# Side value blocks of a decode kernel: eight-way loads from the Pool engine's queue instead of five-way loads from SP's

## The chip, the core and the metric

The kernel runs on one core of a Trainium2 chip. A core has a matrix engine (PE), a vector engine (DVE), a scalar engine (ACT), a general engine (POOL, also called GpSimd), a sync engine (SP) that here only issues transfers, and sixteen DMA engines that move data from the device's memory into the on-chip memory of 128 partitions. The metric is the device time of one execution in microseconds (us); lower is better.

## The reference

Two layers over two sequences, one new token each: layer norm, grouped-query attention over a cache of 32768 keys, residual, layer norm, a gated feed-forward (ReGLU), residual. All in 32-bit floats.

```
def A(x, k_cache, v_cache, wq, wo):          # Hq 32, Hkv 8, rep 4, Dh 128, Sk 32768, D 512
    q = (x @ wq).reshape(B, Sq, Hq, Dh).transpose(0, 2, 1, 3)
    k, v = jnp.repeat(k_cache, rep, axis=1), jnp.repeat(v_cache, rep, axis=1)
    scores = jnp.einsum("bhqd,bhkd->bhqk", q, k) * (Dh ** -0.5)
    o = jnp.einsum("bhqk,bhkd->bhqd", softmax(scores, axis=-1), v)
    return o.transpose(0, 2, 1, 3).reshape(B, Sq, Hq * Dh) @ wo
def B(x, W_gate, W_up, W_down):              # F 1792
    gate, up = x @ W_gate, x @ W_up
    return ((gate * (gate > 0)) * up) @ W_down
x = x + A(_layernorm(x), k_cache, v_cache, wq, wo);  x = x + B(_layernorm(x), W_gate, W_up, W_down)
x = x + A(_layernorm(x), k_cache, v_cache, wq, wo);  x = x + B(_layernorm(x), W_gate, W_up, W_down)
```

The two caches are 1 GB of the 1.1 GB that an execution reads: 16 pairs of a head group and a sequence, each with 16.8 MB of keys and 16.8 MB of values in each layer. The output is two rows of 512 numbers.

## The kernel before

The order of all work is written out by hand; no scheduler changes it. A layer has sixteen turns, one for each pair of key-value head and sequence. Turn `i` scores its keys (`keys(i)`, matmuls `sc`, line 218), then multiplies the values of turn `i - 1` (`values(i - 1, ...)`, matmuls `acc`, line 304) while the softmax of turn `i` runs on DVE and ACT. The second layer walks the turns in the reverse order, and takes a part of the first layer's last keys and values from on-chip memory, where they were kept (`kept_k`, `kept_v`).

Nearly all loads go into one large buffer, `arena`, of 221 units of 256 numbers in each partition. `take(width)` gives a piece of it, `done(...)` returns it; the piece that was returned longest ago is used first, so that a load waits for the work which used that piece last and for the load that filled it. All loads are issued by SP, in the order of the program (line 76). SP waits until the first load in its queue may start; whatever stands behind waits with it.

Keys and values of a turn are eight pages (`j` 0 to 7) of 4096 numbers a partition, 2 MB each. In most turns four pages come with one transfer of 64 KB a partition; in the last two turns of a layer values come page by page. A transfer over 128 partitions is split evenly over the sixteen DMA engines, and each engine takes its shares in the order of issue, so that a page is there when the last engine has finished.

A page of values is eight blocks of 512 numbers a partition: each block holds 128 keys by 4 chunks, and is multiplied by 16 columns of transposed probabilities `pT`. In one turn of each layer, turn 14 (`SIDE_TURNS`), page 3 is loaded without its last three blocks (width 2560), and these three blocks come apart, out of an array `side` that the host has laid out anew from the same values: two transfers (`load_side`, line 292) over 20 partitions each, whose source has an outer dimension of 5. Their keys stand in other partitions than in the page. `side_keys` (lines 269 to 273) therefore makes a second set of transposed probabilities for them, and `v_side` (line 280) multiplies them: ten matmuls behind those of page 3.

Pool has little to do: two powers for the norm of the queries (line 193), and the clearing of a few buffers.

Of the kernel before, what the change touches and what calls it, by code (L numbers as in the profile page):

```python
# [7 lines left out]
F32 = mybir.dt.float32  # L8
# [4 lines left out]
P = 128  # L13
D = 512
# [3 lines left out]
NG = HKV * NB  # L18
NT = 8
# [5 lines left out]
NLAYER = 2  # L25
# [3 lines left out]
PIECE = 256  # L29
PAGE = 4096  # L30
HALF = 4
UNITS = 221
TOP = 192
SCRATCH = 64


KEPT_PAGES = (4, 5, 6)
# [8 lines left out]
C_SAME, C_MEAN, C_SEL, C_PAIR, C_SIDE, C_ONE, C_MHALF, C_END = 0, 128, 160, 192, 224, 225, 226, 228  # L46


@with_exitstack
def attention_reglu_decode(ctx: ExitStack, tc: tile.TileContext, x, k, v, wq, wo, wgu, wd, consts, side, out):  # L50
    nc = tc.nc
    sb = ctx.enter_context(tc.tile_pool(name="sb", bufs=1))
# [21 lines left out]
    def load(src, top=False):  # L74
        t = take(src.shape[-1], top, False)
        nc.sync.dma_start(t[0], src)
# [38 lines left out]
    selh = sel[:, :16]  # L115
    col = sel[:, :NB]
    pair = cst[:, C_PAIR : C_PAIR + 32]
    side_rows = cst[:, C_SIDE : C_SIDE + 1]
# [122 lines left out]
    def soft_tail(L, n, aside=False):  # L241
        p, rs = red_of.pop(n)
        pT = take(2 * D)
        for B in range(2):
            nc.vector.transpose(pT[0][:, B * D : (B + 1) * D], p[0][:, B * D : (B + 1) * D])  # L245
        if aside:
            side_of[n] = side_keys(p[0])
        done(p)
        sm = small(f"sm{L}_{n}")
        nc.tensor.matmul(sm[:, 0:1], same, rs, start=True, stop=True)  # L250
        linv = one()
        nc.vector.reciprocal(linv, sm[:, 0:1])  # L252
        pT_of[n], linv_of[n] = pT, linv
# [2 lines left out]


    def side_keys(p):
        W = SIDE_CHUNKS * 32
        t = take(2 * W)  # L260
        at = SIDE_PAGE // 2 % 2 * D + (SIDE_PAGE % 2 * 8 + 8 - SIDE) * 32

        def windows(rows):
            return bass.AP(rows.tensor, rows.offset + at, [rows.ap[0], [SIDE_ROWS, SIDE_CHUNKS], [1, 32]])

        def chunks(rows):
            return rows.rearrange("p (k r) -> p k r", r=32)

        nc.gpsimd.memset(t[0][64:, W:], 0.0)
        nc.vector.transpose(chunks(t[0][:, :W]), windows(p))  # L270
        for c in (0, 32):
            nc.vector.transpose(chunks(t[0][c : c + 32, W:]), windows(p[64 + c : 96 + c]))
        nc.vector.tensor_scalar_mul(t[0], t[0], side_rows[:, 0:1])
        return t

    def v_side(n, vt):
        t = side_of.pop(n)
        J = SIDE_PAGE // 4
        for k in range(2 * SIDE_CHUNKS):
            nc.tensor.matmul(  # L280
                acc[32 * (k % 4) : 32 * (k % 4) + 16, :],
                t[0][:, 32 * k + 16 * J : 32 * k + 16 * J + 16],
                vt[:, k * D : (k + 1) * D],
                start=False, stop=False,
            )
        done(t)

    def load_side(at):
        W = 2 * SIDE_CHUNKS * D
        t = take(W, False, False)  # L290
        for c in range(2):
            nc.sync.dma_start(t[0][32 * c : 32 * c + SIDE_ROWS], side[at, c, :, : 4 * W].rearrange("e (r f) -> e r f", r=4))
        return t


# [1 line left out]
    def v_tile(n, j, vt, first, last, blocks):  # L297
        pT = pT_of[n][0].rearrange("p (b m r) -> p b m r", m=16, r=32)
        parts = 4 // len(blocks) if len(blocks) < 4 else 1
        for at, ch in enumerate(blocks):  # L300
            J, B, m = j // 4, j // 2 % 2, j % 2 * 8 + ch
            for e in range(parts):
                c, w = (ch + e * len(blocks)) % 4, D // parts
                nc.tensor.matmul(  # L304
                    acc[32 * c : 32 * c + 16, e * w : (e + 1) * w],
                    pT[:, B, m, 16 * J : 16 * J + 16],
                    vt[:, at * D + e * w : at * D + (e + 1) * w],
                    start=first and ch < 4, stop=last and blocks[-1] == 7 and at >= len(blocks) - 4,
                )

    acs_of = {}
# [78 lines left out]
    for L in range(NLAYER):  # L390
        last = L == NLAYER - 1
        seq = list(range(NG)) if L % 2 == 0 else list(range(NG - 1, -1, -1))

        def keys(i):
            n = seq[i]
            if i < NG - 1:
                place_queries(i + 1, seq[i + 1])
            if last and i == 0:
                loads = list(kept_k)
                kept_k.clear()  # L400
            else:
                loads = pages(k, n, not (last and i == 1))
            for j, t in enumerate(loads):
                k_tile(L, i, n, j, t[0])
                if not last and i == NG - 1:
                    kept_k.append(t)
                else:
                    done(t)
                if last and i == 0:
                    yield  # L410
                if j == 1 and i >= 1:
                    soft_tail(L, seq[i - 1], i - 1 in SIDE_TURNS)
                if j == 2 and i >= 2:
                    head_out(L, seq[i - 2])
                    if i % 2 == 1:
                        project(load(wo[seq[i - 2] // NB], True), i == 3, False)


        def values(i, soft):
            n = seq[i]  # L420
            whole = (j for j in ())
            if i == NG - 1:
                pieces = [(j, 0, 8, None) for j in range(NT - 1)]
                pieces += [(NT - 1, h, h + 2, None) for h in range(0, 8, 2)]
                if not last and KEPT_FROM < 8:
                    pieces[KEPT_PART : KEPT_PART + 1] = [(KEPT_PART, 0, KEPT_FROM, None), (KEPT_PART, KEPT_FROM, 8, None)]
            elif last and i == 0:
                pieces = kept_v[1:] + kept_v[:1]
                pieces += [(j, 0, 8 if j != KEPT_PART else KEPT_FROM, None) for j in range(NT) if j not in KEPT_PAGES]
                kept_v.clear()  # L430
            else:
                pieces = [(j, 0, 8, None) for j in range(NT)]
                if i in SIDE_TURNS:
                    pieces[SIDE_PAGE] = (SIDE_PAGE, 0, 8 - SIDE, None)
                elif i < NG - 2:
                    whole = pages(v, n, True)
            for at, (j, lo, hi, t) in enumerate(pieces):
                t = t or next(whole, None) or load(v[n, j // HALF, :, j % HALF * PAGE + lo * D : j % HALF * PAGE + hi * D])
                v_tile(n, j, t[0], at == 0, j == NT - 1, range(lo, hi))
# [6 lines left out]
                if i in SIDE_TURNS and j == SIDE_PAGE:  # L446
                    t_side = load_side(len(SIDE_TURNS) * L + SIDE_TURNS.index(i))
                    v_side(n, t_side[0])
                    done(t_side)
# [73 lines left out]
```

## Time and profile before

| | |
|---|---|
| median of three runs | 2586.75 us (2586.34 to 2587.0) |
| the profiled execution | 2585.52 us, span of its instructions 2583.7 us |
| read from memory | 1105.39 MB, 428 GB/s over the span |
| packets of the DMA engines | 31446, of which 31204 from SP's queue, 75 of instructions |
| chain that ended last | DMA 69%, PE 22%, unknown 8% |
| SP waited at the side pieces (line 292) | 42.4 us once for values, 10.5 for keys, 4.8 and 2.1 for PE |

Times in the profile count from the first instruction of the span. A row of a table by stretches gives the stretch, its length, the busy time of each engine with the number of instructions, the clock that PE was granted, the mean busy share of the sixteen DMA engines (1.00 is all of them, all of the time; a packet counts where it starts, so short stretches can lie a little beside the truth), and the GB/s. In rows of work, "SPq" is SP issuing a transfer, "PEld" is PE loading weights, and "[2.41 <-DMA arena<-side]" says that the engine sat idle for 2.41 us until that transfer had landed. A PE matmul of the program is two in the profile.

### The profile page before, as it was taken

The numbers are of one execution on the slowest core, as the hardware profiler recorded it, in microseconds if no ns is written. First come the engines' busy times: TensorE is split into PE (matmuls) and PEld (weight loads), VectorE is DVE, ScalarE is ACT, GpSimd is POOL, SyncE is SP. The second block draws the span as 40 slices with busy tenths as digits, with TensorE's granted clock in tenths as the row PEclk, the third lists the DMA queues.
The fourth block names the chain that finished last, engine by engine and source line by source line (L and its number), as shares of the span: only waits on it lengthen the run. The fifth ranks groups of instructions, "written<-read, shape, count | busy, mean of one in ns | idle before, by whom it ended". The sixth has DMA issues, their size and how long they took to land.

```text
span 2583.7 us, 20190 instructions
## 1 busy us (share of the span) xinstructions
PE 1322.4 (51%) x9588; PEld 351.7 (14%) x9588; DVE 148.4 (6%) x357; ACT 40.9 (2%) x67; POOL 2.4 (0%) x10
## 2 busy tenths in 40 slices
PE   3554554455455445545685454445445544554465
PEld 1111111111111111111121111111111111111111
DVE  0000000000000000000010000000000000000000
ACT  0000000000000000000000000000000000000000
POOL 0000000000000000000000000000000000000000
PEclk9777777777777777777777777777777777777787
DMA  9999999999999999999999999999999999999999
GB/s 423 436 426 433 436 430 433 437 428 435 431 436 427 436 437 427 434 434 403 414 387 438 428 433 435 434 430 436 431 430 437 433 426 437 435 430 434 431 424 376
DMA packets 31446, 1106.75 MB, mean 428 GB/s; under 512 B 3500, under 2 KB 3764, under 8 KB 6836
## 3 DMA queue, kind: packets, MB, share of 16 engines
q1 hardware_dynamic: 31204, 1105.34, 99.5%
q8 instruction: 75, 1.23, 0.2%
q10 hardware_dynamic: 160, 0.12, 0.0%
q14 instruction: 7, 0.06, 0.0%
HBM read 1105.39 MB, written 0.07 MB: 428 GB/s over the span
## 4 chain that ended last, share of the span: by engine, by line
DMA 69%; PE 22%; another core or an unknown queue 8%; DVE 0%; issue 0%; ACTq 0%; SPq 0%; POOL 0%; DVEq 0%; POOLq 0%
DMA arena<-k 45%; DMA arena<-v 21%; PE sc L218 14%; PE acc L304 5%; DMA cst<-consts 1%; DMA arena<-wgu 1%; PE qp L186 1%; PE po L326 1%; DMA arena<-wq 1%; PE op L166 1%; PE gu L345 0%; PE dn L371 0%; PE mp L232 0%; PE sm L250 0%
## 5 line engine op out<-in xcount | busy, mean ns | idle before, releaser
L304 PE MATMUL acc<-arena 128*16 128x512 f32 (+1 forms) x4116 | 593.0, 727 | 598.5 <-DMA arena<-v 598.5
L218 PE MATMUL sc<-arena,qz 128*32 128x512 f32 x4096 | 591.6, 730 | 592.6 <-DMA arena<-k 592.6
L218 PEld LDWEIGHTS sc<-arena,qz 128*32 128x32 f32 x4096 | 143.4, 130 | 987.8 <-issue 664.9
L304 PEld LDWEIGHTS acc<-arena 128*16 128x16 f32 x4116 | 118.5, 109 | 1023.1 <-issue 512.4
L228 DVE TENSOR_REDUCE stat<-sc 128x1 f32<-128x1024 f32 x32 | 39.2, 1225 | 662.4 <-PE sc L218 662.4
L238 ACT ACTIVATE arena<-sc,stat 128x1024 f32<-128x1024 f32 x32 | 35.6, 1113 | 2360.2 <-DVE stat L235 2308.2
L320 DVE TENSOR_SCALAR arena<-acc,stat 128x512 f32<-128x512 f32 (+1 forms) x38 | 24.8, 665 | 810.6 <-PE acc L304 810.6
L245 DVE STREAM_TRANSPOSE arena<-arena 128x512 f32<-128x512 f32 x64 | 41.5, 687 | 2.4 <-ACT arena L238 2.4
L326 PE MATMUL po<-cst,arena 128*128 128x4 f32 x256 | 34.7, 258 | 2.1 <-DVE arena L320 2.1
L326 PEld LDWEIGHTS po<-cst,arena 128*128 128x128 f32 x256 | 31.9, 195 | 26.7 <-issue 23.5
L252 DVE RECIPROCAL stat<-sm 128x1 f32<-128x1 f32 x32 | 5.3, 166 | 415.4 <-PE sm L250 415.4
L345 PE MATMUL gu<-arena 128*32 128x448 f32 x128 | 22.7, 836 | 9.5 <-DMA arena<-wgu 9.2
L235 DVE TENSOR_REDUCE stat<-mp 128x1 f32<-128x32 f32 x32 | 6.1, 191 | 350.1 <-PE mp L232 350.1
L186 PE MATMUL qp<-arena 128*32 128x512 f32 x128 | 22.7, 822 | 5.7 <-DMA arena<-wq 3.0
L166 PE MATMUL op<-arena,oT 128*2 128x128 f32 x512 | 18.3, 287 | 4.1 <-DVE oT L329 4.1
L232 PEld LDWEIGHTS mp<-arena,cst 128*128 128x128 f32 x64 | 13.1, 256 | 52.1 <-issue 49.6
L145 PE MATMUL meana<-cst,stat 128*128 128x32 f32 x4 | 1.0, 341 | 35.5 <-DMA cst<-consts 35.0
L232 PE MATMUL mp<-arena,cst 128*128 128x32 f32 x64 | 16.9, 353 | 3.5 <-DVE arena L231 3.5
L250 PEld LDWEIGHTS sm<-stat,cst 128*128 128x128 f32 x64 | 9.5, 188 | 28.4 <-issue 28.4
L166 PEld LDWEIGHTS op<-arena,oT 128*2 128x2 f32 x512 | 12.3, 87 | 6.4 <-DVE oT L329 5.5
L250 PE MATMUL sm<-stat,cst 128*128 128x1 f32 x64 | 12.2, 260 | 0.0
L329 DVE COPY oT<-po 128x4 f32<-128x4 f32 x32 | 5.1, 161 | 76.4 <-PE po L326 76.4
(56 smaller groups left out, 94.1 us busy)
## 6 DMA issues: line engine op xcount, KB each, us to landing
arena<-v SPq DMA_DIRECT2D x31, 2048.0 KB, 27.7
arena<-wo SPq DMA_DIRECT2D x16, 1024.0 KB, 51.2
arena<-k SPq DMA_DIRECT2D x8, 2048.0 KB, 16.8
arena<-wq SPq DMA_DIRECT2D x8, 1024.0 KB, 8.5
arena<-wgu SPq DMA_DIRECT2D x8, 896.0 KB, 7.9
arena<-wgu SPq DMA_DIRECT2D x4, 1792.0 KB, 21.0
arena<-v SPq DMA_DIRECT2D x8, 512.0 KB, 34.2
arena<-wd SPq DMA_DIRECT2D x4, 1024.0 KB, 8.7
```

The costliest lines, as they stand in the source:

```text
L166: nc.tensor.matmul(tot[32 * c : 32 * c + rows.shape[-1], :P], rows, w[:, c * P : (c + 1) * P], start=start, stop=stop)
L186: nc.tensor.matmul(qp[32 * c : 32 * c + 32, B, :], xT[:, kt, :], t[0][:, c * D : (c + 1) * D], start=kt == 0, stop=kt == KT - 1)
L218: nc.tensor.matmul(sc_of[n][32 * c : 32 * c + 32, B, :], qz[:, i % 2, 28 - 4 * j : 60 - 4 * j], kt[:, ch * D : (ch + 1) * D], start=j == 0 ...
L228: nc.vector.tensor_reduce(m1, sc_of[n], AX.XY, ALU.max)
L232: nc.tensor.matmul(mp[:, :32], same, mt[0], start=True, stop=True)
L238: nc.scalar.activation(p[0], sc_of[n].rearrange("p a b -> p (a b)"), AF.Exp, bias=nm[:, 0:1], scale=1.0, accum_out=rs)
L245: nc.vector.transpose(pT[0][:, B * D : (B + 1) * D], p[0][:, B * D : (B + 1) * D])
L250: nc.tensor.matmul(sm[:, 0:1], same, rs, start=True, stop=True)
L304: nc.tensor.matmul(acc[32 * c : 32 * c + 16, e * w : (e + 1) * w], pT[:, B, m, 16 * J : 16 * J + 16], vt[:, at * D + e * w : at * D + (e + ...
L320: nc.vector.tensor_scalar_mul(acs[:, at : at + w], acc[:, at : at + w], linv[:, 0:1])
L326: nc.tensor.matmul(po[:, :REP], acs[0][:, t * P : (t + 1) * P], selh[:, 4 * t : 4 * t + 4], start=t == 0, stop=t == 3)
L345: nc.tensor.matmul(gu[32 * j : 32 * j + 32, s, :FS], xT[:, kt, :], t[0][:, j * FS : (j + 1) * FS], start=kt == 0, stop=kt == KT - 1)
```

## The change

Turn 14 of each layer now leaves the last three blocks out of two pages, 3 and 7, so that there are six side blocks a layer. They keep the keys' partitions modulo 64: partitions 0 to 63 hold the blocks of the page's lower half and, beside them, those of its upper half. For the lower half `pT` is used as it is, and for the upper half `side_keys` transposes two small pieces of 32 x 96.

The side pieces are now issued by Pool (`nc.gpsimd.dma_start`), whose transfers go through a queue that software on Pool fills. Each page's side blocks come in two transfers over 32 partitions, whose source has an outer dimension of 8. In front of each stands a transfer of a few numbers into a buffer of its own, `turned`, by `steer`: with 13 groups the first time, with 8 each time after. The change counts on Pool's queue giving the groups of a transfer to as many DMA engines, starting behind the one where the transfer before ended: 13 engines, then 8 for side data, then always 8 and 8, so that the side data is always on the same eight.

The scratch memory that such a queue needs grows from 64 to 512, and `arena` loses one unit. The column of constants that `side_keys` used falls away.

```
-UNITS = 221
+UNITS = 220
-SCRATCH = 64
+SCRATCH = 512
-SIDE_TURNS = (14,)
-SIDE_PAGE, SIDE = HALF - 1, 3
-SIDE_ENGINES, SIDE_ROWS, SIDE_CHUNKS, SIDE_GAP = 5, 20, 5, 64
+SIDE_TURN = NG - 2
+SIDE_PAGES, SIDE = (3, 7), 3
+SIDE_ROWS, SIDE_GAP, BEFORE, AROUND = 64, 64, 13, 8
...
     def side_keys(p):
...
-        nc.gpsimd.memset(t[0][64:, W:], 0.0)
-        nc.vector.transpose(chunks(t[0][:, :W]), windows(p))
+        B, m = SIDE_PAGES[0] // 2 % 2, SIDE_PAGES[0] % 2 * 8 + 8 - SIDE
+        at = B * D + m * 32
+        t = take(SIDE * 32)
         for c in (0, 32):
-            nc.vector.transpose(chunks(t[0][c : c + 32, W:]), windows(p[64 + c : 96 + c]))
-        nc.vector.tensor_scalar_mul(t[0], t[0], side_rows[:, 0:1])
+            nc.vector.transpose(t[0][c : c + 32], p[64 + c : 96 + c, at : at + SIDE * 32])
         return t
...
+    turned = sb.tile([P, 4], F32, name="turned")
+    whole_turn = [BEFORE, AROUND]
+    def steer():
+        n = whole_turn[0] if len(whole_turn) > 1 else AROUND
+        if len(whole_turn) > 1:
+            whole_turn.pop(0)
+        few = consts[: 5 * n, :4].rearrange("(e r) f -> e r f", r=5)[:, :4]
+        nc.gpsimd.dma_start(turned[: 4 * n], few)
     def load_side(at):
-        W = 2 * SIDE_CHUNKS * D
-        t = take(W, False, False)
-        for c in range(2):
-            nc.sync.dma_start(t[0][32 * c : 32 * c + SIDE_ROWS], side[at, c, :, : 4 * W].rearrange("e (r f) -> e r f", r=4))
+        t = take(2 * SIDE * D, False, False)
+        for c in range(SIDE_ROWS // 32):
+            steer()
+            nc.gpsimd.dma_start(t[0][32 * c : 32 * c + 32], side[at, c, :, : 8 * SIDE * D].rearrange("e (r f) -> e r f", r=4))
         return t
...
+                aside = i == SIDE_TURN and j in SIDE_PAGES
                 t = t or next(whole, None) or load(v[n, j // HALF, :, j % HALF * PAGE + lo * D : j % HALF * PAGE + hi * D])
+                if aside:
+                    t_side = load_side(len(SIDE_PAGES) * L + SIDE_PAGES.index(j))
+                    v_side(n, j, t_side[0])
+                    done(t_side)
                 v_tile(n, j, t[0], at == 0, at == len(pieces) - 1, range(lo, hi))
```

On SP's queue, at turn 14 of the first layer, the difference is this piece; the names are the loads' target and source, and the widths are partitions by numbers:

```order
 L76 DMA arena<-v 128x4096 x3
 L76 DMA arena<-v 128x2560
-L292 DMA arena<-side 20x1x5120 x2
-L76 DMA arena<-v 128x4096 x7
+L76 DMA arena<-v 128x4096 x3
+L76 DMA arena<-v 128x2560
+L76 DMA arena<-v 128x4096 x3
 L76 DMA arena<-v 128x2048 x2
```

The side pieces have left SP's queue, and page 7 has become shorter as page 3 was.

Pool's queue before, from the first layer's norm of the queries to the end, with what each instruction waits for ("DMAHW" counts transfers of SP and ACT, "DMASW" those of Pool):

```order
L193 TENSOR_TENSOR stat<-stat,cst 128x2 [waits DMAHW3_49,DVE_49]
L269 MEMSET arena 64x160 [waits DVE_49,PE_49,Pool_49]
L193 TENSOR_TENSOR stat<-stat,cst 128x2 [waits DVE_49,Activation_49,Pool_49]
L269 MEMSET arena 64x160 [waits DMAHW2_49,DMAHW3_49,DVE_49,DMAHW4_49,PE_49,Pool_49]
```

And Pool's queue after the change, through the first layer to the first side piece of the second; `turned` is the small target of `steer`:

```order
L192 TENSOR_TENSOR stat<-stat,cst 128x2 [waits DMAHW3_49,DVE_49]
L287 DMA turned<-consts 52x1x4
L293 DMA arena<-side 32x1x3072 [waits DMAHW5_49,DMAHW4_49,PE_49]
L287 DMA turned<-consts 32x1x4 [waits DMASW0_49]
L293 DMA arena<-side 32x1x3072
L287 DMA turned<-consts 32x1x4 [waits DMASW2_49]
L293 DMA arena<-side 32x1x3072 [waits DMAHW3_49,DMAHW2_49,PE_49]
L287 DMA turned<-consts 32x1x4 [waits DMASW4_49]
L293 DMA arena<-side 32x1x3072
L192 TENSOR_TENSOR stat<-stat,cst 128x2 [waits DVE_49,Activation_49,Pool_49]
L287 DMA turned<-consts 32x1x4 [waits DMASW6_49]
L293 DMA arena<-side 32x1x3072 [waits DMAHW1_49,DMAHW5_49,DMASW1_49,PE_49]
```

Four side pieces a layer now stand here, each behind a small transfer, and the second layer's norm of the queries stands behind the first layer's four. The first piece of a pair waits for its buffer: in the first layer the first pair has a buffer whose last use was an output-weight product of PE during `keys(15)`, and the second pair one that the trimmed page 3 has used. Page 4 of turn 14 now goes into the piece that page 0 of the same turn has left.

More of the change, by code (lines that the diff above doesn't have):

```diff
@@ L271, in side_keys, with v_side @@
+        at = B * D + m * 32
+        t = take(SIDE * 32)
         for c in (0, 32):
-            nc.vector.transpose(chunks(t[0][c : c + 32, W:]), windows(p[64 + c : 96 + c]))
-        nc.vector.tensor_scalar_mul(t[0], t[0], side_rows[:, 0:1])
-        return t
[L276 to L279, printed above, removed]
+            nc.vector.transpose(t[0][c : c + 32], p[64 + c : 96 + c, at : at + SIDE * 32])
+        return t
+    def v_side(n, j, vt):
+        J, B, m = j // 4, j // 2 % 2, j % 2 * 8 + 8 - SIDE
+        low = pT_of[n][0].rearrange("p (b m r) -> p b m r", m=16, r=32)[:SIDE_ROWS, B, m : m + SIDE]
+        high = side_of[n][0].rearrange("p (m r) -> p m r", r=32)[:SIDE_ROWS]
+        for k in range(2 * SIDE):
+            c = k % 4
@@ L280, in v_side @@
             nc.tensor.matmul(
-                acc[32 * (k % 4) : 32 * (k % 4) + 16, :],
-                t[0][:, 32 * k + 16 * J : 32 * k + 16 * J + 16],
-                vt[:, k * D : (k + 1) * D],
+                acc[32 * c : 32 * c + 16, :],
+                (low if k < SIDE else high)[:, k % SIDE, 16 * J : 16 * J + 16],
+                vt[:SIDE_ROWS, k * D : (k + 1) * D],
                 start=False, stop=False,
             )
-        done(t)
+    turned = sb.tile([P, 4], F32, name="turned")
@@ L307, in v_tile @@
                     vt[:, at * D + e * w : at * D + (e + 1) * w],
-                    start=first and ch < 4, stop=last and blocks[-1] == 7 and at >= len(blocks) - 4,
+                    start=first and ch < 4, stop=last and at >= len(blocks) - 4,
                 )
@@ L445, in values @@
                     soft_max(L, soft)
[L446 to L449, printed above, removed]
+            if i == SIDE_TURN:
+                done(side_of.pop(n))
             evacuate(L, n, i == NG - 1)
@@ L479 @@
     cst[:, C_PAIR : C_PAIR + 32] = np.equal.outer(rows // 4, np.arange(32))
-    cst[:, C_SIDE] = (rows < 64) & (rows % 32 < SIDE_ROWS)
     cst[:, C_ONE] = 1.0 / D
```

34 lines of the change are left out of this document (11 added, 23 removed).

## The prediction

> **What bounds the kernel now.** I read the page's DMA lines first, then the table of busy time by stretches, then the order of work at the two places where that table falls below full.
>
> ```profile
> PE 1322.4 (51%) x9588; PEld 351.7 (14%) x9588; DVE 148.4 (6%) x357; ACT 40.9 (2%) x67; POOL 2.4 (0%) x10
> q1 hardware_dynamic: 31204, 1105.34, 99.5%
> q8 instruction: 75, 1.23, 0.2%
> q10 hardware_dynamic: 160, 0.12, 0.0%
> ```
> No compute engine is busy for much over half the span; the sixteen DMA engines are, nearly all of it. The next rows are stretches in us; the last two columns are the mean busy share of the sixteen DMA engines and GB/s.
>
> ```profile
> 30.00:1218.00 1188.00, 595.77 (x4314) 159.00 (x4318) 63.97 (x148) 18.07 (x30) 0.92 (x2) 0.74 1.00 432
> 1218.50:1227.00 8.50, 5.36 (x49) 1.16 (x43) 1.27 (x3) 1.20 (x2) 0.00 (x0) 1.00 0.73 276
> 1219.00:1222.00 3.00, 2.93 (x26) 0.66 (x18) 0.77 (x3) 1.20 (x2) 0.00 (x0) 1.00 0.49 206
> 1222.30:1225.30 3.00, 1.41 (x16) 0.36 (x16) 0.00 (x0) 0.00 (x0) 0.00 (x0) 1.00 0.83 294
> 1227.00:1286.00 59.00, 37.76 (x208) 6.88 (x212) 2.07 (x5) 0.00 (x0) 0.00 (x0) 0.71 1.00 422
> 1289.00:1292.00 3.00, 1.90 (x20) 0.91 (x20) 1.11 (x4) 0.00 (x0) 0.00 (x0) 0.88 0.64 239
> 1296.00:1310.00 14.00, 11.16 (x58) 3.55 (x58) 1.41 (x8) 0.54 (x1) 0.00 (x0) 0.62 0.90 315
> 1340.00:1345.00 5.00, 5.00 (x52) 1.35 (x48) 0.12 (x1) 0.00 (x0) 0.00 (x0) 1.00 0.92 344
> 1400.00:2400.00 1000.00, 492.48 (x3562) 130.01 (x3558) 50.62 (x114) 14.45 (x24) 0.00 (x0) 0.73 1.00 433
> 2570.00:2571.00 1.00, 0.07 (x4) 0.07 (x8) 0.00 (x0) 0.00 (x0) 0.00 (x0) 1.00 0.98 399
> 2572.00:2576.00 4.00, 2.48 (x16) 0.45 (x12) 1.27 (x2) 0.00 (x0) 0.00 (x0) 0.50 0.80 329
> 2577.00:2578.00 1.00, 1.00 (x12) 0.28 (x8) 0.00 (x0) 0.00 (x0) 0.00 (x0) 0.50 0.56 207
> ```
> Through a layer every DMA engine is busy, at 433/16 = 27.1 GB/s each, so only bytes or idle engines can buy time there. The rows at the layer's end show idle engines, and how many. At 1219-1222 the share is 0.49: eight of sixteen have run out while eight still work on what was issued before. At 1222.3-1225.3 it is 0.83, thirteen: five of the idle eight have got the side pieces, three have nothing. In the last layer the share falls from 0.98 to 0.80 at about 2571 (three out of work) and only from 2577 on do the other thirteen end: the three are about 6.5 us ahead. So eight engines gain some 6.5 us on the other eight in a layer; the side pieces take that lead from five of them. Idle time, as length times missing share: 2.3 us (1218.5-1227), 1.1 (1289-1292), 1.4 (1296-1310), 0.4 (1340-1345), together 5.2 us of all sixteen in the middle; and three engines for 6.5 us at the end.
>
> The order of issue and of the matmuls around the first place:
>
> ```profile
> 1176.27 0.33 SPq L76 DMA_DIRECT2D arena<-v  x1
> 1221.10 1.70 SPq L292 DMA_DIRECT2D arena<-side  x2
> 1222.84 45.48 SPq L76 DMA_DIRECT2D arena<-v  x16
> 1194.51 1.05 PE L166 MATMUL op<-arena,oT 128*2 128x128 f32 x32 [0.26 <-DVE oT L329]
> 1217.86 1.89 PE L304 MATMUL acc<-arena 128*16 128x512 f32 x16
> 1220.02 1.91 PE L304 MATMUL acc<-arena 128*16 128x512 f32 x16
> 1226.98 1.89 PE L304 MATMUL acc<-arena 128*16 128x512 f32 x10 [1.18 <-DMA arena<-v]
> 1231.28 2.76 PE L280 MATMUL acc<-arena 128*16 128x512 f32 x20 [2.41 <-DMA arena<-side]
> SPq L292 <- DMA arena<-v: 42.4, 1, 42.4
> arena<-side SPq DMA_DIRECT2D x4, 400.0 KB
> 2547.48 23.41 DMA arena<-wgu
> ```
> SP issues nothing from 1176.6 to 1221.1, because the next thing in its queue is the side pair, whose buffer lies over the first two value pages and is free when the second has been used (1220.02 + 1.91); the waits of SP put 42.4 us down to that pair. The early engines run dry at 1218.7 meanwhile. The last row is of the chain that ends the kernel: the reglu weights' last DMA, behind which come only short steps.
>
> **The change, part by part.** A piece of 20 partitions is 400 KB on five engines, so the two of a layer cost each of the five 2 x 409,600 / 5 / 27.1 = 6.05 us, against the lead of 6.5. Leaving three of eight blocks out of one page relieves all sixteen by 48 KB, 1.8 us.
>
> After the change six blocks are left out, 96 KB or 3.6 us for every engine, and come back as 1,536 KB on eight engines, 7.3 us each. If those are the eight early ones, a layer changes by -1.8 us for the late eight, by -0.6 for the five (7.3 - 3.6 against 6.05 - 1.8), and by +5.4 for the three that had no side work; lead and load then differ by 7.3 - 6.5 = 0.8 us.
>
> Last layer: the chain there is the weights' DMA, so the end follows the slowest engine: between -0.6 and -1.8; I take -1.1, as the thirteen end within a microsecond or so of each other.
>
> First layer: the first side pair no longer waits in SP's queue. Its buffer was last used by the output weights of the turn, whose use is the row at 1194.51, over at 1195.6, so Pool can issue it 20 us before the early engines run dry; its 3.6 us carry them from 1218.7 to 1222.3. The next value page waits for the first page alone (1217.86 + 1.89 = 1219.75) and moves from about 1221.2, as the side pieces moved some 1.3 us behind their issue. That stall of 2.3 us goes. The five engines, which took side data from 1222.5 to 1228.6 while the rest took up the next page at 1225.3, are no longer 3.3 us late when the layer's last values land; all sixteen come within 1 or 2 us, and the 1.1 us at 1289-1292, in which the others wait for the page that these five bring, goes too. Behind it the weights are issued as the chain of matmuls frees buffers; it starts earlier by about what the engines do, so I count half to two thirds of its 1.4 us: 0.9. What is late next there is this chain. First layer: -4.3, between -2.3 (the first stall alone) and -5.2 (all idle time).
>
> Small parts. Eight transfers of the kind that move the cursor, 832 and 512 bytes of data: q10, a second data queue with 160 small packets, cost 0.0%, so nothing. The padding that is no longer loaded is 32 KB a layer over sixteen engines, 0.15 us in both. PE has 12 side products for 10 and three fewer of the others: at 594 ns a record nothing, and PE has room (37.76 of 59 us). One unit less of scratch moves the small tiles, not the three 64-unit buffers.
>
> ```profile
> L280 PE MATMUL acc<-arena 128*16 128x512 f32 x40 | 6.3, 594 | 2.4 <-DMA arena<-side 2.4
> L270 DVE STREAM_TRANSPOSE arena<-arena 128x160 f32<-128x160 f32 x2 | 0.6, 303 | 0.0
> L273 DVE TENSOR_SCALAR arena<-arena,cst 128x320 f32<-128x320 f32 x2 | 0.8, 386 | 0.2
> L193 POOL TENSOR_TENSOR stat<-stat,cst 128x2 f32<-128x2 f32 x2 | 1.4, 693 | 1222.1 <-DVE stat L160 1222.1
> 1328.73 0.69 POOL L193 TENSOR_TENSOR stat<-stat,cst 128x2 f32<-128x2 f32 x1 [1183.15 <-DVE stat L160]
> ```
> DVE loses 0.303 + 0.386 us a layer, off the path (6% busy); Pool loses a memset. New is that the second layer's 693 ns of L193, which the queries need and which ran at 1328.73, stands on Pool behind the first layer's four side pieces, the last of which waits for the trimmed page's matmuls (1226.98 + 1.89): 100 us of cover. The second pair is used only after three more pages of 4.9 us (2 MB at 27.1 GB/s an engine), so Pool's issuing, even at several us a piece, is hidden.
>
> The price that no row shows is that of a Pool-issued packet. Each early engine gets 196.6 KB a layer. From below: at the rate of q1 there is no surcharge. From above: q8, the other queue with large packets, took 0.2% of 16 x 2583.7 for 75 packets of 16 KB, 1.1 us each where 27.1 GB/s makes 0.6; at that ratio of 1.8 the 7.3 us become 13.2. Nearest is q1, the same data from the same memory into the same buffers; I charge a tenth of the upper end, 0.6 us, at the end, and 0.1 in the middle. A gain from it I exclude: the engines are at 1.00.
>
> [...]
>
> **Sum.** -4.3 - 1.1 - 0.15 + 0.7 = -4.85, say -4.7. The profiled execution took 2585.52 (span 2583.7); it would take 2580.8. It lies 1.2 below the median of 2586.75, so for the median 2582.0.
>
> **Rivals.**
> The wrong engines (slower). The pieces land on the right eight only if Pool's cursor stands where 13 and then 8 steps suppose, in every execution; nothing in the trace numbers the engines or shows a cursor. One late engine among the eight is enough: it carries +3.6 where it had -1.8, so it ends 5.4 us later in the last layer, and about 2 later than the five do now in the first (5.4 - 3.3): +7.4, 2594. For it: a cursor left over from the last execution would not start at zero. Against: that exactly eight engines are early fits one run of eight, and the five that take side data now are all among them (0.49, then 0.83).
>
> Dear packets (slower or the same). With x us of surcharge a layer the end moves by x and the middle by nearly x: no gain left at 2.7 us a layer (1.37 times q1's time), slower by over 0.2% from 5.3 (1.7 times); at q8's ratio 2593. For it stands q8 alone.
>
> All sixteen. If the pieces are spread over every engine, nobody's lead is used: the late eight end 1.8 us later than now, the first layer gains about 3.3 - 1.8 = 1.5: 2587. [...]
>
> No lead at that time (slower). The pieces go out at 1196, at a share of 1.00. Were the lead not there yet, each would take its eight engines 7.3 us where sixteen take 3.6: +3.6 a layer, 2594. The lead of 6.5 us speaks against it. [...]
>
> The chain holds. If the stretch from 1289 to 1345 takes as long as now whatever the engines do, only the last layer and part of the 2.3 us stay: 2585.
>
> **How the numbers follow.** A measurement of this kernel can tell about 0.2%, 5.2 us, from no change; the forecast lies just inside that. Right engines and cheap packets 0.66, from 2579.5 (all idle time, -1.8 at the end) to 2584: 0.33 faster, 0.33 within. The chain 0.10 and all sixteen 0.05: within. Wrong engines 0.12: slower 0.10, within 0.02. Dear packets 0.05: slower 0.03, within 0.02. No lead 0.02: slower. Together faster 0.33, within 0.52, slower 0.15. The range from 2579.5 to 2589 leaves out the wrong engines, the dearest packets and the missing lead, 0.15.
>
> **What would show it.** Right: the share at the first layer's end stays above 0.9 where it was 0.49, no engine is idle before the last microsecond or two at the end, and no wait of PE names the side pieces. Wrong: eight or so engines idle for over 6 us at either end (wrong engines), the Pool queue's share above its 3.1 MB's part of the bytes, 0.28% (dear packets), or 0.64 still standing before the reglu weights (the chain).

## The result and the profile after

The changed kernel takes 2604.21 us (median of four runs, 2603.1 to 2606.27), the kernel before 2586.55 (2583.76 to 2587.0): a ratio of 1.0071, 95% interval 1.0054 to 1.0089. It is 17.7 us slower, where the prediction said 4.7 faster. The profiled execution took 2603.1 us, its span is 2601.3.

The span and the two large DMA queues of the kernel after (packets, MB, share of sixteen engines):

```profile
span 2601.3 us, 20195 instructions
q1 hardware_dynamic: 31104, 1102.13, 99.0%
q0 software_dynamic: 896, 3.15, 0.4%
```

The engines are as busy as before; the bytes are the same, less 0.06 MB (1102.13 + 3.15 against 1105.34). So the same transfers took longer. The table by stretches of the kernel before, at five places around the side pieces (last two columns: share of busy DMA engines, GB/s):

```profile
1190.00:1218.00 28.00, 15.79 (x154) 5.43 (x150) 0.33 (x2) 0.00 (x0) 0.00 (x0) 0.82 0.98 418
1218.00:1236.00 18.00, 10.48 (x84) 2.22 (x72) 1.66 (x3) 1.20 (x2) 0.00 (x0) 1.00 0.86 346
1236.00:1262.00 26.00, 18.34 (x98) 3.85 (x102) 2.07 (x5) 0.00 (x0) 0.00 (x0) 0.64 1.01 428
2475.00:2495.00 20.00, 17.66 (x138) 4.29 (x131) 1.66 (x3) 1.21 (x2) 0.00 (x0) 0.90 1.00 425
2495.00:2515.00 20.00, 11.48 (x77) 2.76 (x75) 1.59 (x3) 0.00 (x0) 0.00 (x0) 0.91 1.01 429
```

And of the kernel after, with three more stretches: the place of the old stall, the end of the first layer's values, and the end of the last layer's weights:

```profile
1190.00:1218.00 28.00, 15.90 (x138) 5.29 (x134) 0.33 (x2) 0.00 (x0) 2.16 (x4) 0.73 0.98 365
1218.00:1236.00 18.00, 13.08 (x92) 2.57 (x84) 1.66 (x3) 1.20 (x2) 0.00 (x0) 0.81 1.00 411
1219.00:1222.00 3.00, 3.00 (x30) 0.82 (x22) 1.47 (x2) 0.00 (x0) 0.00 (x0) 1.00 1.01 420
1236.00:1262.00 26.00, 12.86 (x70) 1.97 (x69) 0.00 (x0) 0.00 (x0) 1.61 (x3) 0.74 0.99 354
1295.00:1298.00 3.00, 1.76 (x24) 0.39 (x24) 0.00 (x0) 0.00 (x0) 0.00 (x0) 1.00 0.27 110
2475.00:2495.00 20.00, 12.20 (x82) 3.01 (x82) 1.47 (x2) 0.00 (x0) 2.16 (x4) 0.66 0.98 341
2495.00:2515.00 20.00, 9.49 (x52) 1.48 (x53) 0.19 (x1) 1.21 (x2) 0.00 (x0) 0.66 1.00 369
2592.00:2595.00 3.00, 2.13 (x16) 0.34 (x16) 0.16 (x1) 0.00 (x0) 0.00 (x0) 1.00 0.15 59
```

Three things stand there. The stall is gone: 0.49 at 1219-1222 has become 1.01. While side pieces move, all engines are busy and yet move less: 365 for 418, 354 for 428, 341 for 425, 369 for 429 GB/s. As length times missing rate that is 3.6 + 4.5 = 8.0 us in the first layer and 4.0 + 2.8 = 6.8 in the last, against some 2.8 us (18 x (411 - 346) / 420) won where the stall was. Not all of the 4.5 in the stretch from 1236 is due to the choice of engines and partitions: four of the runs below, in which the side pieces slow nothing down elsewhere (the two on engines 0 to 7, and those on 8 to 15 and on 13 to 4 with their own partitions), move only 395 to 405 there too, which is 1.4 to 2.0 of the 4.5 us, and no run tells why. And at both ends a few engines work on alone: 0.27 of sixteen is four of them, 0.15 two or three.

The orders on Pool show when the pieces went out, and the norm of the second layer's queries (line 192) marks how far the first layer had come:

```profile
1196.77 0.55 POOL L293 DMA_DIRECT2D arena<-side  x1 [1155.26 <-PE op L165]
1197.84 0.56 POOL L293 DMA_DIRECT2D arena<-side  x1
1213.39 0.54 POOL L287 DMA_DIRECT2D turned<-consts  x1 [15.00 <-DMA turned<-consts]
1236.84 0.54 POOL L293 DMA_DIRECT2D arena<-side  x1 [22.91 <-PE acc L305]
1333.09 0.72 POOL L192 TENSOR_TENSOR stat<-stat,cst 128x2 f32<-128x2 f32 x1 [94.47 <-DVE stat L159]
2461.23 0.54 POOL L293 DMA_DIRECT2D arena<-side  x1 [1126.87 <-PE sc L217]
```

The first pair went out when the prediction said, at 1196.8, the second at 1236.8, 8 us behind the end of the trimmed page's matmuls in the kernel before (1226.98 + 1.89); soon after each the GB/s fall. The norm ran at 1333.09, 4.4 us later than the 1328.73 of before; the span is 17.6 us longer, so the second layer lost the other 13.2.

### The profile page after: what moved, and what is told of

Read it like the earlier page. It is cut to its first block, busy times and chain, and to the rows that moved or that the text cites. A ratio compares the mean times of both kernels' runs of the same rounds, so it can differ in the third digit from the quotient of the medians.

```text
span 2601.3 us, 20195 instructions
## 1 busy us (share of the span) xinstructions
PE 1326.0 (51%) x9584; PEld 349.2 (13%) x9584; DVE 147.0 (6%) x353; ACT 40.9 (2%) x67; POOL 10.8 (0%) x24
## 3 DMA queue, kind: packets, MB, share of 16 engines
q1 hardware_dynamic: 31104, 1102.13, 99.0%
q0 software_dynamic: 896, 3.15, 0.4%
## 4 chain that ended last, share of the span: by engine, by line
DMA 63%; PE 25%; another core or an unknown queue 12%; DVE 0%; issue 0%; SPq 0%; ACTq 0%; POOL 0%; DVEq 0%; POOLq 0%
DMA arena<-k 49%; PE sc L217 16%; DMA arena<-v 11%; PE acc L305 6%; DMA cst<-consts 1%; DMA arena<-wgu 1%; DMA arena<-wd 1%; DMA arena<-wq 1%; PE po L327 1%; PE qp L185 1%; PE op L165 1%; PE gu L346 0%; PE mp L231 0%; PE sm L249 0%
## 5 line engine op out<-in xcount | busy, mean ns | idle before, releaser
L346 PE MATMUL gu<-arena 128*32 128x448 f32 x128 | 20.9, 775 | 11.4 <-DMA arena<-wgu 9.7
L249 PE MATMUL sm<-stat,cst 128*128 128x1 f32 x64 | 12.2, 261 | 0.0
```

Source lines behind the costliest of these rows:

```text
L346: nc.tensor.matmul(gu[32 * j : 32 * j + 32, s, :FS], xT[:, kt, :], t[0][:, j * FS : (j + 1) * FS], start=kt == 0, stop=kt == KT - 1)
```

## The experiments

I held three theories. A: a group of four partitions has one way in, which in a large transfer is fed by one engine alone; a side piece that another engine writes there makes two engines share it, and both are slow while they count as busy. B: packets of Pool's queue are dear. C: there is no contention, some of the eight engines are only late ones. A late engine is one of those without the lead of some 6.5 us, an early one has it. No row of the profile numbers the engines, says which partitions one writes, or shows a cursor. The numbers here are my assumption, which the change counts on: engine `g` or `8 + g` for group `g` of the lower or the upper 64 partitions in a large transfer, Pool's cursor as described with the change, and SP's side pieces from engine 0 on. What speaks for it are rates: in the stretches 2475-2495 and 2495-2515 the kernel before and the ten runs whose side pieces keep to these partitions move 416 to 431 GB/s, and the three kernels that leave them 300 to 403. "Sharing" below is short for side pieces that leave them; that there is a way in which two engines share is theory A's guess, and no row shows it. Times of before are those on the chip of the runs compared: 2583.15 for the first four, 2583.14, 2583.32 and 2583.01 for the others.

**Eight engines from 0.** The first small transfer is left out, so that the cursor starts the side data at engine 0.

```
-    whole_turn = [BEFORE, AROUND]
+    whole_turn = [0, AROUND]
...
+        if n == 0:
+            return
```

> The changed kernel without its first small transfer, so that the cursor stands at 0 and every side piece goes to engines 0 to 7 instead of 13 to 4. Group g of a piece (partitions 4g to 4g+3, or 32+4g to 35+4g) then goes to engine g, which writes the same partitions in the large transfers. Theory A, shared way into a group's partitions (a piece whose groups lie on other engines than the large transfers use for these partitions makes two engines share one way in, and both slow down): no contention here; GB/s while side pieces move stays near 420 to 430 at a share of 1.00, where the changed kernel shows 326 to 332; three late engines (5 to 7) carry 3.6 us more than before at each layer's end, so about 2592 to 2595. Theory B, dear packets (the Pool queue's packets cost more wherever they go): GB/s while they move is as low as in the changed kernel, 2602 to 2610. Theory C, wrong engines without contention (13 to 4 holds late engines): a spread of ends of 12 us or so, which moves with the engines, and GB/s above 420 while the pieces move in either kernel.

**Eight engines from 8.**

```
-SIDE_ROWS, SIDE_GAP, BEFORE, AROUND = 64, 64, 13, 8
+SIDE_ROWS, SIDE_GAP, BEFORE, AROUND = 64, 64, 8, 8
```

> The changed kernel with 8 in place of 13 in the first small transfer: side pieces on engines 8 to 15. Every group's partitions belong to an engine of 0 to 7 in the large transfers, so by theory A all eight pairs share a way in, as in the changed kernel: GB/s of 320 to 380 while the pieces move, 2600 to 2612. Theory B: the same as e1_eight_0 to within 2 us. Theory C: GB/s above 420 while the pieces move, and an end given by engines 8 to 12, 2592 to 2596.

Measured: from 0 2589.32 us, ratio 1.0026 (1.0015 to 1.0036); from 8 2614.1, ratio 1.0123 (1.0102 to 1.0143). From 0, two stretches of the last layer, one at its end, and Pool's queue:

```profile
2475.00:2495.00 20.00, 13.36 (x102) 3.36 (x98) 1.66 (x3) 1.21 (x2) 1.62 (x3) 0.84 1.00 422
2495.00:2515.00 20.00, 15.71 (x94) 2.55 (x86) 0.00 (x0) 0.00 (x0) 0.00 (x0) 0.81 1.01 428
2577.00:2581.00 4.00, 2.13 (x16) 0.34 (x16) 1.07 (x3) 0.00 (x0) 0.00 (x0) 1.00 0.13 52
q0 software_dynamic: 864, 3.15, 0.3%
```

From 8:

```profile
2475.00:2495.00 20.00, 3.46 (x28) 0.85 (x24) 0.00 (x0) 0.00 (x0) 0.55 (x1) 0.60 0.95 307
2495.00:2515.00 20.00, 9.25 (x78) 2.33 (x74) 1.66 (x3) 1.20 (x2) 1.61 (x3) 0.84 1.01 300
```

The two differ in nothing but the number that moves the cursor, and are 25 us apart. From 0 the rate is as good as before (422, 428), from 8 it falls to 300 at a share of 1.01. So the first small transfer decides where the side data goes, as the change counts on; Pool's queue is not dear in itself (its share is 0.3% here, 0.4% in the changed kernel, for the same bytes); and, the partitions being the same in both, it matters which engines write them. From 0 two engines (0.13) work on alone at the end: two of 0 to 7 are late ones. I had expected three, and 2592 to 2595; from 8, 2600 to 2612 and at least 320 GB/s, and sharing cost more than that.

**Pool's queue for the old pieces.** The kernel before with its five-way pieces issued by Pool, and a small transfer of 11 groups between them.

```
-            nc.sync.dma_start(t[0][32 * c : 32 * c + SIDE_ROWS], side[...])
+            steer()          # 11 groups, none ahead of the first piece
+            nc.gpsimd.dma_start(t[0][32 * c : 32 * c + SIDE_ROWS], side[...])
```

> The kernel before, with its two side pieces a layer of 20 partitions issued by Pool instead of SP: five groups on engines 0 to 4 (a small transfer of 11 groups between two pieces brings the cursor back to 0), the same bytes on the same engines as before. Arena two units smaller. Theory A: nothing contends, the pieces leave SP's queue, so the stall of five to eight engines at the first layer's end shrinks: 2582 to 2587. Theory B: the five engines' 6.05 us of packets a layer become about 10 or more, 2592 to 2600. Theory C says nothing of it: as before, 2584 to 2588.

**SP's queue for the new pieces.** The changed kernel with its pieces issued by SP, without small transfers.

```
-            steer()
-            nc.gpsimd.dma_start(t[0][32 * c : 32 * c + 32], side[...])
+            nc.sync.dma_start(t[0][32 * c : 32 * c + 32], side[...])
```

> The changed kernel with its side pieces issued by SP and without the small transfers: eight groups, which I take to be on engines 0 to 7, through the hardware queue. Theory A: no contention, three late engines with 3.6 us more; SP's queue has the pieces in order again: 2591 to 2597, within 4 us of e1_eight_0. Theory B: 8 us or more faster than e1_eight_0. Theory C: as e1_eight_0.

Measured: 2583.95 us, ratio 1.0004 (0.9994 to 1.0013), and 2589.66, ratio 1.0027 (1.0017 to 1.0038). The old pieces cost the same by either queue, and so do the new ones on engines 0 to 7 (2589.32 by Pool). B is out. With the old pieces on Pool's queue the stall stayed, which I had expected to shrink: Pool waited for the same buffer, issued the pair at 1222.09, and the share at 1219-1222 was 0.50.

**The same engines, the partitions that are theirs.** Eight engines from 8 again, but the pieces go to partitions 64 to 127.

```
-            nc.gpsimd.dma_start(t[0][32 * c : 32 * c + 32], side[...])
+            nc.gpsimd.dma_start(t[0][SIDE_ROWS + 32 * c : SIDE_ROWS + 32 * c + 32], side[...])
```

> The changed kernel with the cursor moved by 8 instead of 13, so that the side pieces go to engines 8 to 15 as in the run e2_eight_8, but written to partitions 64 to 127 instead of 0 to 63. Engine 8+g then writes group g of the upper half, which is the group that it writes in every large transfer as well. If two engines share one way into a group of partitions when a piece lands beside its own engine (theory A), this run has no sharing: GB/s at 2475 to 2515 goes from the 300 of e2_eight_8 to 415 to 430, and the time from 2614 to 2588 to 2596 (some of the engines 8 to 15 are late ones, and carry 3.7 us more than before). If engines 8 to 15 are bad in themselves or only late (theory C), partitions change nothing: 2610 to 2616, and 300 to 310 GB/s. Dear packets of Pool's queue (B), already against the runs so far, would give the same as e2_eight_8 too.

Measured: 2592.11 us, ratio 1.0033 (1.002 to 1.0045).

```profile
2475.00:2495.00 20.00, 14.06 (x98) 3.36 (x98) 1.66 (x3) 1.21 (x2) 2.16 (x4) 0.76 1.00 421
2495.00:2515.00 20.00, 11.41 (x70) 1.88 (x70) 0.00 (x0) 0.00 (x0) 0.00 (x0) 0.82 1.01 428
2574.00:2577.00 3.00, 1.71 (x16) 0.42 (x16) 0.00 (x0) 0.01 (x1) 0.00 (x0) 1.00 0.61 253
2578.00:2583.00 5.00, 2.84 (x28) 0.67 (x32) 1.27 (x2) 0.00 (x0) 0.00 (x0) 1.00 0.39 161
```

The same engines and bytes; 307 and 300 GB/s have become 421 and 428, and 22 us are gone. That is as theory A had it (415 to 430); C (300 to 310) is out as the whole cause. The kept traces hold the time of every DMA packet, and show the slowing directly: a side packet of 12,288 bytes took 0.46 us on the mean from 0, 0.69 from 8 and 0.47 here, and 0.58 in the changed kernel. There SP's own packets of 16,384 bytes slowed down as well, from 0.62 us before to 0.80 in the stretch from 1190 to 1218. The end also counts the late engines: at 0.61 ten of sixteen work, so six of 0 to 7 have ended early, and at 0.39 six of 8 to 15 are left. Six early ones in the first half, two in the second: eight, as the prediction had read.

**The changed kernel's own engines, each on its own partitions.** Engines 13 to 15 write partitions 84 to 95 and 116 to 127 in place of 20 to 31 and 52 to 63; 0 to 4 write what they wrote before the change.

```
-            nc.gpsimd.dma_start(t[0][32 * c : 32 * c + 32], side[at, c, ...])
+            nc.gpsimd.dma_start(t[0][84 + 32 * c : 96 + 32 * c], side[at, c, 5:, ...])
+            nc.gpsimd.dma_start(t[0][32 * c : 32 * c + 20], side[at, c, :5, ...])
```

> The changed kernel on the same eight engines (13, 14, 15, 0 to 4), with each engine writing its own groups: engines 0 to 4 write partitions 0 to 19 and 32 to 51 as before the change, and engines 13 to 15 partitions 84 to 95 and 116 to 127 in place of 20 to 31 and 52 to 63. Each piece of 32 partitions has become two, of three and of five engines; the probabilities of both halves are transposed anew and masked, since the keys stand in other partitions. Engines, bytes and queue are those of the changed kernel. This tells the choice of engines from the sharing of ways in. Theory A: GB/s while the pieces move goes from 341 to 369 back to 420 to 430, and the time from 2601 to 2580 to 2590. Where within that: if all eight are early ones, the forecast's sum holds, 2578 to 2582; if one or two of 13 to 15 are late, each late one ends 5.4 us behind the early ones' old end, 2587 to 2590, and the share near the end falls to 0.06 or 0.13 for some 3 to 5 us. Theory C (sharing is nothing, the engines are wrong): 2600 to 2605 as the changed kernel.

**Three other engines.** The same with 10 to 12 in place of 13 to 15; the keys' probabilities do not move along, so that other numbers are computed.

> The same as e9_own_13 with engines 10, 11 and 12 in place of 13, 14 and 15, each writing its own groups (partitions 72 to 83 and 104 to 115), and small transfers of 10, 3 and 5 that move the cursor. The keys' probabilities are not moved along, so that the side pieces are multiplied by other keys' numbers; bytes, instructions and order are the same. It tells which of engines 8 to 15 are early: the mirror run e5_upper_8 showed two early ones among 8 to 15. If the two are among 13 to 15, this run has three late engines (a share of 0.19 near the end) and takes 2587 to 2590; if among 10 to 12, it ends with one late engine, and e9_own_13 is the one with three. GB/s while the pieces move 420 to 430 in either case (A).

Measured: 2590.35 us, ratio 1.0027 (1.0016 to 1.0038), and 2591.32, ratio 1.003 (1.0018 to 1.0042). With 13 to 15, the last layer, its end, and the norm of the second layer's queries:

```profile
2475.00:2495.00 20.00, 13.86 (x98) 3.41 (x98) 1.66 (x3) 1.21 (x2) 3.25 (x6) 0.76 1.00 416
2495.00:2515.00 20.00, 13.11 (x70) 2.26 (x70) 0.00 (x0) 0.00 (x0) 0.00 (x0) 0.79 1.02 429
2581.00:2586.00 5.00, 3.04 (x40) 0.88 (x40) 1.76 (x3) 0.00 (x0) 0.00 (x0) 1.00 0.14 54
1330.01 0.72 POOL L193 TENSOR_TENSOR stat<-stat,cst 128x2 f32<-128x2 f32 x1 [93.29 <-DVE stat L160]
```

With 10 to 12, the end:

```profile
2579.00:2584.00 5.00, 2.69 (x28) 0.44 (x24) 1.47 (x3) 0.00 (x0) 0.00 (x0) 1.00 0.19 78
```

The sharing is taken away and 1.0071 becomes 1.0027: the sharing cost 0.44% or 11.4 us, give or take some 5 by the two intervals. The side packets are back at 0.47 us, and the norm runs 3.1 us earlier than in the changed kernel. What is left, 7.0 us, comes with two engines at work alone (0.14) for over five microseconds: two of 13 to 15 are late ones. All of 10 to 12 are (0.19, three engines). Both times lie at or just above the 2587 to 2590 that I had expected.

**Sharing alone.** The kernel before, SP's queue and engines 0 to 4, with the target of the side pieces moved by one group of partitions. The values then stand beside the wrong keys' probabilities, so that other numbers are computed.

```
-            nc.sync.dma_start(t[0][32 * c : 32 * c + SIDE_ROWS], side[...])
+            nc.sync.dma_start(t[0][32 * c + 4 : 32 * c + 4 + SIDE_ROWS], side[...])
```

> The kernel before, and nothing changed but the target partitions of its side pieces: 4 to 23 and 36 to 55 in place of 0 to 19 and 32 to 51. Engines 0 to 4, bytes, SP's queue and order stay; each of the five now writes the next group of four partitions, which in the large transfers is its neighbour's. The values then stand one group beside their keys' probabilities, so other numbers are computed. Theory A: GB/s drops while the pieces move (1222 to 1240, 2457 to 2500). In the changed kernel against e9_own_13 sharing cost 0.44 per cent, 11.4 us, or 5.7 a layer at 7.3 us of side data an engine; with 6.05 us of data that is 4.7 a layer, of which the early engines' spare half microsecond hides little and engine 5, late and now shared, nothing: 3 to 5 a layer, 2589 to 2593. Theory C: no change, 2582 to 2584.

Measured: 2595.2 us, ratio 1.0046 (1.0032 to 1.006): 12.2 us for an offset of four partitions. The first of these rows is the kernel before, the second and third the moved target:

```profile
1226.00:1246.00 20.00, 11.51 (x66) 2.03 (x70) 0.00 (x0) 0.00 (x0) 0.00 (x0) 0.77 1.00 420
```
```profile
1226.00:1246.00 20.00, 10.70 (x46) 2.11 (x46) 0.00 (x0) 0.00 (x0) 0.00 (x0) 0.66 0.96 369
2475.00:2495.00 20.00, 13.67 (x99) 3.44 (x99) 1.66 (x3) 1.21 (x2) 0.00 (x0) 0.76 0.97 383
```

The rate falls from 420 to 369 and from 425 (shown above) to 383. I had expected 2589 to 2593; engines, queue, bytes and order are those of before, so what did it is which partitions the same engines write, and it cost more than I took from the difference of two other runs.

**The stall alone.** The kernel before with `load_side` ahead of the turn's pages, and its matmuls behind page 0.

```
+            if i in SIDE_TURNS:
+                t_side = load_side(...)
...
-                if i in SIDE_TURNS and j == SIDE_PAGE:
-                    t_side = load_side(...)
+                if i in SIDE_TURNS and at == 0:
                     v_side(n, t_side[0])
```

> The kernel before, five-way side pieces on SP's queue, with load_side moved ahead of the turn's value pages and its matmuls behind those of page 0 instead of page 3. Only the stall in SP's queue is taken away. My prediction priced that stall at 2.3 us of a sum of 4.85. If the first layer's gain was real and contention ate it (A), this kernel is 1 to 3 us faster than before and the share at 1218 to 1227 goes from 0.73 to above 0.9. If the chain of matmuls sets the end of the first layer whatever the engines do, it is within 0.5 us of before, with the stall gone all the same and the idle time standing later, at 1285 to 1300.

> The kernel of e6_early once more, since its gain of 1.65 us had an interval that touches none. If the stall in SP's queue is worth what my prediction took for its lower bound of the first layer (2.3 us), the ratio to before is 0.9990 to 0.9995 again, 2580.5 to 2582; if the first run was chance, it is 1.0.

Measured: 2581.49 us, ratio 0.9991 (0.9982 to 1.0), and again 2581.31, ratio 0.9989 (0.9981 to 0.9998). This version is 1.7 us faster than the kernel before, just above what can be told. Its issue of the side pieces, two of the stretches that the prediction shows of before, and the norm, from the first of the two runs:

```profile
1170.94 1.70 SPq L292 DMA_DIRECT2D arena<-side  x2
1218.50:1227.00 8.50, 8.31 (x78) 2.08 (x70) 1.66 (x3) 1.21 (x2) 0.00 (x0) 1.00 0.93 366
1289.00:1292.00 3.00, 2.35 (x34) 1.55 (x34) 0.80 (x4) 0.00 (x0) 0.00 (x0) 0.54 1.01 406
1325.84 0.70 POOL L193 TENSOR_TENSOR stat<-stat,cst 128x2 f32<-128x2 f32 x1 [1179.59 <-DVE stat L160]
```

SP issues the pair 50 us earlier, 0.73 has become 0.93, and 0.64 at 1289-1292 has become 1.01. The norm runs at 1325.84, where it ran at 1328.73; part of that lies in the level of the two profiles, since before took 2583.14 us beside this run and 2586.55 beside the changed kernel.

**Six engines in place of five,** and the same with the early issue.

```
-SIDE_ENGINES, SIDE_ROWS, SIDE_CHUNKS, SIDE_GAP = 5, 20, 5, 64
+SIDE_ENGINES, SIDE_ROWS, SIDE_CHUNKS, SIDE_GAP = 6, 24, 4, 64
```

> The kernel before with its side pieces over six engines (0 to 5) in place of five: SIDE_ENGINES, SIDE_ROWS, SIDE_CHUNKS 6, 24, 4, so that there is no padding and each engine gets 2 x 65,536 bytes, 4.8 us instead of 6.05. All six are aligned. If engine 5 is one of the early ones, the time is the same to 1 us less, and the share in the last microseconds is as before. If engine 5 is late, it ends 4.8 - 1.8 = 3.0 us later at the end of the last layer and about 2 in the first: 3 to 5 us slower than before, and one engine is seen alone at work at the end (a share of 0.06).

> The two edits together: six engines, and the pieces ahead of the turn's pages. If both hold (engine 5 early, the stall worth its time) 1 to 3.5 us faster than before. If only the stall counts, the same as e6_early plus up to 5. If neither, no difference from before to slower by 5.

Measured: 2587.33 us and 2587.47, ratio 1.0018 both (1.0009 to 1.0026 and 1.0009 to 1.0027). The first one's end:

```profile
2577.00:2581.00 4.00, 3.84 (x36) 1.30 (x32) 0.69 (x1) 0.00 (x0) 0.00 (x0) 0.57 0.08 29
```

One engine (0.08) is left at work alone: engine 5 is a late one, and 3.0 us more on it in each layer cost 4.2. The smaller buffer (4096 numbers a partition in place of 5120) fell on another place, which came free earlier: in the first of the two runs SP issued the pair at 1196.76, in time for the idle engines, and the share at 1219-1222 is 0.93 in place of 0.49. So the stall is gone in both, which is why the early issue adds nothing, and the 4.2 us are what is left after that gain.

## Why the prediction was wrong

*The idle engines and the stall: right.* Eight were idle at 1219-1222 and the stall went (0.49 to 1.01). Alone it was worth 1.7 us, of the 2.3 that the prediction took as the least for the first layer. Eight early engines with a lead of some 6.5 us is right too: in the run on 13 to 15 the two late ones work alone from about 2580 to 2587 (0.14 throughout 2581-2586).

*"If those are the eight early ones": they are not.* Two of 13, 14 and 15 are late. The prediction had this as the rival of the wrong engines, at 0.12, with one late engine enough for +7.4; with the sharing taken away the same engines cost 7.0. The size was right and the chance was too low. "That exactly eight engines are early fits one run of eight" was no evidence: eight early engines need not be neighbours, and the five that were known (0 to 4) said nothing of the other three. The rule that the end follows the slowest engine held: with two late engines among the eight it came out at 6.2 and 7.0 us, with three at 8.0, with six at 9.0.

*"Nearest is q1, the same data from the same memory into the same buffers": failed, and most of the loss lies here.* The term was +0.7 for both layers and is some 11.4, or 5.7 a layer, nearly the 5.9 that q8's ratio gave as the upper end; that they meet is chance. The dear thing was not the packet of Pool's queue, as the rival of dear packets had it: with the pieces on engines 0 to 7 it took 0.46 us, about what 27.1 GB/s make of its 12,288 bytes (0.45), and 0.58 only where the pieces land in the changed kernel. The old pieces cost the same by either queue, and the new ones on engines 0 to 7 too. What differs from q1 is the place. By the numbering above, the five engines of the old side pieces wrote the partitions that they write in q1's large transfers as well (425 and 429 GB/s beside those of the last layer), and four partitions further on the same pieces cost 12.2 us; starting at engine 13 instead, group 0 goes to engine 13, and every group of a piece lands in another engine's partitions (341 to 369). The prediction costed a side packet by its engine's time alone and never asked which partitions each engine writes; the trace of before could not show it, since by that numbering nothing in that kernel crossed.

The runs show that the pairing of engines and partitions counts: with the pieces on engines 8 to 15 the core moves 300 GB/s when they go to partitions 0 to 63, and 428 when they go to 64 to 127. The price of a wrong pairing is the 11.4 us here, and 12.2 for the moved target; what it is in the hardware that slows both down, no run shows. The 7.0 us that are left without sharing come from two engines (0.14), not from all eight.

*The first layer, -4.3, and the last, -1.1: not reached.* In the first layer 8.0 us of lost rate, 6.0 to 6.6 of them by sharing, stand against 2.8 won at the stall; 5.2 by that, and the norm of the queries was 4.4 late. In the last, 6.8 of lost rate and the prediction's 5.4 for a late engine make 12.2 by estimate, where the span lost 13.2. The idle time at 1289-1292, which was to go, came back as 0.27 at 1295-1298; with the stall alone taken away it did go (1.01), which fits the prediction's reading that the five engines with late side pieces made it.

*Small parts: right.* Pool waited 15 and 20 us for two of its small transfers and 23 for a buffer, and no wait of PE names a side piece; the norm waited for DVE, not for Pool's queue.

*Of the signs to look for, one held and one misled.* The sign of the wrong engines showed: at the end some thirteen of sixteen stood idle for about 6 us (0.15 at 2592-2595). The other misled: a share above 0.28% for Pool's queue was to mean dear packets, and it read 0.4%. The same queue read 0.3% with the cursor at 0. With the moved target side packets are slow on SP's queue too (one of 20,480 bytes took 1.03 us on the mean, before 0.86), so that the share alone could not tell B from A.

What stays open: which engine of 6 and 7, which of 8 and 9 and which of 13 to 15 is early was not tried, nor a kernel with the right eight, each on its own partitions; so the forecast of -4.7 for that case stands untested but for the stall. Why half the engines fall 6.5 us behind in a layer no run tells.

## What to carry to other kernels

A transfer that is put on a part of the engines may depend on the partitions that it goes to: here the same eight engines left the core at 421 and 428 GB/s with one half of the partitions as target and at 307 and 300 with the other, where side packets (0.69 us for 0.47) ran slow while the engines counted as busy (300 GB/s at a share of 1.01). So try another target, and look at GB/s, not at the share. Before you load idle engines, find out which they are: how many are idle doesn't say, and one late engine among them set the end here (engine 5 alone: 4.2 us). A long wait in an issuing queue could be taken away by issuing earlier, without a new queue (0.73 to 0.93 at 1218.5-1227); a new queue alone did not take it away, since it waited for the same buffer (0.50 at 1219-1222).

## What the runs showed of the hardware

An offset of four partitions in the target of 1.6 MB out of 1105 made a kernel 12.2 us slower. The first small transfer on Pool's queue, left out or of eight groups, moved the time by 25 us with all else equal (2589.32 and 2614.1). If that is by a cursor, as the change counts on, then it seems to begin at the same place in each execution: the eight runs of the kernel without that transfer lie within 4.2 us of each other, though its fifteen transfers of eight groups would leave the cursor eight engines further on; had it been kept, every second execution would have been like the kernel that starts at 8. Packets of Pool's queue and of SP's cost the same here (2589.32 and 2589.66 us).
